# Hashed attention and a gated block on one core: weights prepared in turns, wider sums over keys, another pace

## The chip, the cores and the metric

The kernel runs on one core of a Trainium2 chip. The time is the device time of one launch in microseconds (us), lower is better. A core has five engines with queues of their own, worked off in order: PE (TensorE, matrix products into PSUM), DVE (VectorE), ACT (ScalarE), POOL (GpSimd) and SP (SyncE). Here SP and POOL only issue transfers (DMA), apart from some filling at the start. PEld in the profile is PE's loading of weights.

## The reference

Attention in which a query sees only keys of the same hash bucket (the signs of six projections), then a block `silu(x w_gate) * (x w_val)` times `w_out`. The inputs are float32 from numpy, except that the weights of the second block come out as float64, since `standard_normal * (1 / np.sqrt(...))` keeps that type.

```
batch, n_heads, seq, head_dim = (4, 8, 768, 64)
n_tokens, d_model, d_ff = (3072, 512, 1536)
mask = q_bucket[:, :, :, None] == k_bucket[:, :, None, :]
scores = np.where(mask, scale * q @ k^T, -1e9)
attn = exp(scores - max); attn = attn / (sum + 1e-09)
x = (attn @ v).transpose(0, 2, 1, 3).reshape(B * S, H * D)
g = x @ w_gate
return (g * (1 / (1 + exp(-g))) * (x @ w_val)) @ w_out
```

## The kernel before

**Attention** takes the heads in 16 pairs (4 batches of 4). A pair has 12 units: 2 halves of 384 queries by 6 chunks of 128 keys. For a unit PE makes the scores of both heads (`score`, L461), a second product of bits (`qb`, `kb`) shifts scores of other buckets down, and ACT takes the exponential into a ring of 12 tiles `A`. `attend` (L477) multiplies by `v`. DVE adds the tiles of a half (`add`, L498: one operation for the first two units, one for each later unit, 768 elements each), PE sums `acc` over the partitions (`total`, L512), ACT copies the row, SP spreads it with a transfer (`few`), DVE inverts it (`invert`), two more transfers spread it (`sums`, `r`), and `norm` (L540) multiplies. Results of batch 0 are split into three parts for the gated block (`split`, L238: `high` on ACT, `low` and `diff` on DVE); those of later batches are kept in DRAM (`xram`).

The loop over pairs (L563) writes the order out by hand: transposes on DVE for the next pair and its loads on SP, 12 scores with their sums, `total` of the pair before, `finish(rest)` (with `spread_k`, L408, on DVE), `finish(last)` (the `norm` of two pairs before), `invert`, `begin_pieces`, 6 times `attend`, the splits, 6 times `attend`, `advance_pieces`. After pair 15 it does `finish(last)` and then `total` of pair 15.

**Pieces.** The weights are float64 and are turned on the chip into three float32 parts. There are 36 pieces of 128 x 512: for each of 12 blocks of d_ff a gate and a value piece, and 12 output pieces. Preparing one takes `scale` (two on ACT), `widths` (three on DVE), `round_up` (one on ACT) and `parts` (two on DVE and a write of 768 KB to DRAM, `ram<-stage`). Three stage slots are in turn. Pieces come back for use through a ring of 7 (`bring`, L221). Attention prepares 24 pieces: two per pair in pairs 0 to 3, then one in even and two in odd pairs, none in the last.

**The gated block** is a list of groups (L207): "U" n makes one block of the hidden layer, "D" takes three blocks into the output; a D comes after every third U (U3, then D0, U4, U5, U6, D1 and so on), 48 U and 16 D over four batches. A U has four atoms: gate products and ACT's copy (L674), the correction on DVE (L680) and silu (L682), the same for the value, then the product (L684) and the split into `hid` (L685 on ACT, and on DVE, one atom later, L688 and L690). A D has six atoms, one for each 128 tokens, of nine matmuls and two operations (L721 or L719, then L724). PSUM has four tiles of two banks for all of it. Matmul lines of the gated block show as L632.

After each atom one step of preparing runs (`prepare_on`) and ACT scales ahead (`scale_ahead`). `bring` forces the preparing of a piece that it needs. Before U9 of a batch (the third from its end) all pieces left are prepared, the next batch's results are loaded (`words<-xram`, four on SP over three slots), and their 12 split steps are queued, one per atom after four empty ones: they run in D2, U10 and the first half of U11. `left` holds the last pair's `invert` and `norm`, which run at the 6th and 14th atom.

Of the kernel before, what the change touches and what calls it, by code (L numbers as in the profile page):

```python
# [8 lines left out]
FP32 = mybir.dt.float32  # L9
# [10 lines left out]
def kernel(  # L20
# [157 lines left out]
            for _ in widths(i):  # L178
                pass

    def scale_ahead():
        for i in sorted(added - rounded):
            round_up(i)
        i = progress["scaled"]
        if i < NPIECE and i < progress["kept"] + 2 and i in words:
            scale(i)

    def prepare():
        for i in range(progress["kept"], NPIECE + 1):
            if i < NPIECE and i not in added:  # L190
                load_words(i + 1)
                if i not in staged:
                    scale(i)
                yield from widths(i)
            if i > progress["kept"]:
                round_up(i - 1)
                yield from parts(i - 1)

    preparing = prepare()

    def prepare_on(n):
        for _ in range(n):
            next(preparing, None)

# [16 lines left out]
    def bring(count=1):  # L221
        for _ in range(count):
            i = len(held)
            if i == len(wanted):
                return
            what, n = wanted[i]
            at = place[what, n % NF]
            while progress["kept"] <= at:
                next(preparing)
            pool = ringp[i % sum(RINGS) >= RINGS[0]]  # L230
            held[what, n] = t = pool.tile([P, 3, PIECE], FP32R, tag="ring", name="ring")
            nc.gpsimd.dma_start(t.bitcast(FP32), ram[at].bitcast(FP32))  # L232
# [23 lines left out]
    def attention(scope):  # L256
# [102 lines left out]

        RING = 2 * NCH  # L360
        AW = HQ + 2
        ring = []
        for i in range(RING):
            t = fixed.tile([P, 2, AW], FP32, tag=f"A{i}", name="A")
            nc.gpsimd.memset(t[:, :, HQ:AW], 1.0)
            ring.append(t)
        for t in (sides["k", 0], sides["q", 0], sides["q", 1]):
            nc.gpsimd.memset(t, 0.0)

# [107 lines left out]
        def attend(u):  # L477
# [9 lines left out]
            if c == NCH - 1:  # L487
# [7 lines left out]
                    nc.scalar.activation(mean[n], ps[:, HQ : HQ + 1], AF.Copy, scale=EPS)  # L495
                nc.scalar.copy(xT[n][:, half * HQ : (half + 1) * HQ], ps[:, 0:HQ])

        def add(u):  # L498
            n, half, c = units[u]
            a = weights(u)  # L500
            if c == 1:
                acc[n, half] = att.tile([P, 2, HQ], FP32, tag="acc", name="acc", bufs=4)
                nc.vector.scalar_tensor_tensor(out=acc[n, half], in0=weights(u - 1)[:, :, 0:HQ],  # L503
                                               scalar=S * EPS / P, in1=a[:, :, 0:HQ],
                                               op0=ALU.add, op1=ALU.add)
            elif c > 1:
                nc.vector.tensor_tensor(acc[n, half], acc[n, half], a[:, :, 0:HQ], op=ALU.add)  # L507

        each = 4 * HQ // P
        sums = [dram.tile([P, each], FP32, tag=f"sums{i}", name="sums") for i in range(2)]  # L510
# [15 lines left out]
        def invert(n, few):  # L526
            nc.vector.reciprocal(few, few)
            s = sums[n % 2]
            nc.sync.dma_start(s, few)
            if n == len(pairs) - 1:  # L530
                t = spread[n].rearrange("p (x q) -> p x q", x=2)
            else:
                t = att.tile([P, 2, HQ], FP32, tag="r", name="r")
            flat = s.rearrange("p e -> (p e)").rearrange("(h x t) -> h (x t)", h=2, t=HQ)
            for h in range(2):
                nc.sync.dma_start(t[h * D : (h + 1) * D].rearrange("p x t -> p (x t)"),
                                  flat[h : h + 1].to_broadcast([D, 2 * HQ]))
            return lambda: norm(n, t)

        def norm(n, t):  # L540
            x = xT[n]
            nc.vector.scalar_tensor_tensor(out=x, in0=x, scalar=mean[n],
                                           in1=t.rearrange("p x q -> p (x q)"),
                                           op0=ALU.add, op1=ALU.mult)
            b, pr = pairs[n]
            if b:
                nc.sync.dma_start(kept_x[b, pr], x)
            else:
                splits.extend(split(x, b, pr, even_x))

        steps = front(0)
        rest = []
# [6 lines left out]
        prepare_pair(4)  # L559
        finish(rest)  # L560
        last = []
        splits = []
        for n in range(len(pairs)):  # L563
            u = 2 * NCH * n
            more = n + 1 < len(pairs)
            late = n + 1 > NP
            if n and more:
                steps = front(n + 1)
                if late:
                    prepare_pair(2)  # L570
            for i in range(2 * NCH):
                score(u + i)
                if u + i == 2:
                    prepare_pair(1)
                    finish(rest)
# [12 lines left out]
            finish(rest)  # L588
            finish(last)
            while waiting:  # L590
                last.append(waiting.pop(0)())
            begin_pieces(0 if n == len(pairs) - 1 else 2 if n < NP or n % 2 else 1)
            for c in range(NCH):
                attend(u + c)
            finish(splits)
            for c in range(NCH, 2 * NCH):
                attend(u + c)
            load(n + 2, "v")
            advance_pieces()
            if n >= len(pairs) - 3:  # L600
                bring(2 if n == len(pairs) - 1 else 1)
        finish(last)
        total(len(pairs) - 1)
        left.extend(waiting)

    left = []
# [8 lines left out]
    def gated_block(scope):  # L615
# [47 lines left out]
        def atoms_of(kind, n):  # L663
# [33 lines left out]
            else:  # L697
# [5 lines left out]
                def start(c, js):  # L703
                    if c not in tiles:
                        tiles[c] = two_banks("o")
                    t = tiles[c]
                    cols = slice(c * P, (c + 1) * P)
                    for j in js:
                        for v in range(2):
                            mm(t[:, 0], hs[j][:, v, cols], ws[j][:, v],  # L710
                               j == 0 and v == 0, j == NQ - 1 and v == 1)
                    for j in js:
                        mm(t[:, 1], hs[j][:, 2, cols], ws[j][:, 2], j == 0, j == NQ - 1)

                def end(c):
                    t = tiles.pop(c)
                    if part == 0:
# [6 lines left out]
                    nc.vector.tensor_tensor(accs[c], accs[c], t[:, 1], op=ALU.subtract)  # L724
# [5 lines left out]
                ahead = 4 if n == B * NF // NQ - 1 else 0  # L730
# [10 lines left out]
        tails = []  # L741
        splits = []
        count = [0]
        for kind, n in order:
            if kind == "U":
                b, f = divmod(n, NF)
                if f == NF - NQ and b + 1 < B:
                    while next(preparing, None):
                        pass
                    splits = [None] * 4  # L750
                    for pr in range(NP):
                        t = wordp.tile([P, PIECE, 2], I32, tag="words", name="words")
                        x = t.rearrange("p f w -> p (f w)")[:, 0:S].bitcast(FP32)
                        nc.sync.dma_start(x, kept_x[b + 1, pr])
                        splits += split(x, b + 1, pr, xs[(b + 1) % 2][pr])
            if kind == "D" and n == B * NF // NQ - 1:
                finish(tails)
            for atom in atoms_of(kind, n):
# [4 lines left out]
                if splits:  # L763
                    step = splits.pop(0)
                    if step:
                        step()
                count[0] += 1
                if left and count[0] in (6, 14):
                    left.append(left.pop(0)())
                    left[:] = [f for f in left if f]  # L770
                prepare_on(1)
                scale_ahead()

    with ExitStack() as scope:
        gated_block(scope)
# [32 lines left out]
```

## Time and profile before

| | |
|---|---|
| runs, median (lowest to highest) | 955.48 us (954.71 to 957.72) |
| the profiled execution: time, span | 955.84 us, 954.0 us |
| mean granted clock of PE | 0.993 |
| attention / gated block on PE | until 334.6 us / from 335.28 us |
| a U group, a D group on PE | 8.33 us, 12.28 us |
| DVE operation of 768 / 512 float32 columns | 0.95 to 0.96 / 0.69 us |
| ACT: L674, L682 and L685, scaling (each), round_up | 0.81, 0.85, 0.67, 0.62 us |

The span runs from the first to the last instruction of one execution; its time holds 1.8 us around that. In the timeline a row has its start, its duration, the engine and line, the operation with the tiles it writes and reads, and in brackets how long the engine stood idle before it and who released it. "PE idle" is read there; a busy PE can still be slow, which the granted clock shows (1.00 is full). Operations of DVE and ACT overlap a little in this profile, so the next can start 0.1 us before the one before is shown as ended.

### The profile page before, as it was taken

How to read it: one execution, taken by the hardware profiler on the slowest of the kernel's cores; microseconds unless marked ns; L12 is line 12 of the kernel's file. 1: busy time of each engine (PE TensorE's matmuls, PEld its weight loads, DVE VectorE, ACT ScalarE, POOL GpSimd, SP SyncE). 2: the span in 40 equal slices, each digit the busy share in tenths (PEclk: the TensorE clock that was granted, in tenths of full speed). 3: DMA queues.
4: the chain of work that ended last, by engine and by line, in shares of the span. 5: the costliest groups of instructions: out<-in, count | busy, mean ns of one | idle time of the engine just before them, and what ended most of it. 6: DMA issues, size and time to landing. Idle time of an engine off the chain costs nothing.

```text
span 954.0 us, 14590 instructions
## 1 busy us (share of the span) xinstructions
PE 926.6 (97%) x5413; PEld 726.1 (76%) x5413; DVE 672.6 (71%) x868; ACT 472.6 (50%) x882; POOL 113.2 (12%) x231
## 2 busy tenths in 40 slices
PE   8999999999999979998899999999999999999997
PEld 4444454544444479998699999999999999999996
DVE  5577899899999828796876546775646586446466
ACT  6899777887888535433341331332332421332311
POOL 3011001000111110111011111011111111110100
PEclk9999999999999999999799999999999999999999
DMA  6466767887888597879667465466654646753641
GB/s 167 123 188 175 185 163 197 223 209 186 223 231 219 190 368 264 318 273 352 241 235 287 145 263 188 160 232 235 244 207 162 226 182 203 262 196 133 243 155 67
DMA packets 135798, 203.22 MB, mean 213 GB/s; under 512 B 92912, under 2 KB 100560, under 8 KB 135728
## 3 DMA queue, kind: packets, MB, share of 16 engines
q0 software_dynamic: 27984, 145.64, 42.9%
q1 hardware_dynamic: 106944, 56.46, 22.0%
q8 instruction: 43, 0.70, 0.3%
q10 hardware_dynamic: 800, 0.20, 0.1%
q14 instruction: 27, 0.22, 0.1%
HBM read 162.01 MB, written 39.42 MB: 211 GB/s over the span
## 4 chain that ended last, share of the span: by engine, by line
PE 84%; DVE 5%; DMA 4%; ACT 3%; SPq 2%; issue 1%; DVEq 0%; ACTq 0%
PE a L632 26%; PE o L632 20%; PE sc L471 13%; PE n L632 13%; PE av L485 8%; SPq L296 2%; DVE acc L507 2%; ACT A L474 1%; PE hps L397 1%; DMA few<-row 1%; DMA r<-sums 1%; PE sum L518 1%; DMA ram<-stage 1%; PE tps L384 1%; DMA qb<-qb 1%
## 5 line engine op out<-in xcount | busy, mean ns | idle before, releaser
L632 PE MATMUL a<-xparts,ring 128*128 128x384 f32 x1536 | 283.7, 336 | 5.7 <-ACT g L674 5.1
L632 PEld LDWEIGHTS a<-xparts,ring 128*128 128x128 f32 x1536 | 269.5, 189 | 7.9 <-ACT g L674 5.4
L632 PE MATMUL o<-ring,hid 128*128 128x512 f32 x864 | 201.7, 393 | 7.6 <-ACT g L674 7.6
L632 PEld LDWEIGHTS o<-ring,hid 128*128 128x128 f32 x864 | 163.1, 190 | 42.3 <-ACT g L674 7.9
L474 ACT ACTIVATE A<-sc 128x384 f32<-128x384 f32 x384 | 155.7, 507 | 9.5 <-PE sc L471 9.5
L471 PE MATMUL sc<-qT,kT 64*128 64x384 f32 x768 | 157.9, 488 | 0.0
L632 PE MATMUL n<-xparts,ring 128*128 128x384 f32 x768 | 148.6, 334 | 0.0
L232 POOL DMA_DIRECT2D ring<-ram x144 | 75.9, 529 | 514.1 <-PE n L632 319.6
L632 PEld LDWEIGHTS n<-xparts,ring 128*128 128x128 f32 x768 | 134.5, 188 | 0.0
L507 DVE TENSOR_TENSOR acc<-acc,A 128x768 f32<-128x768 f32 x128 | 122.6, 958 | 13.6 <-DVE acc L503 0.5
L485 PE MATMUL av<-A,vraw 128*64 128x386 f32 (+1 forms) x768 | 127.7, 488 | 0.0
L680 DVE TENSOR_TENSOR v<-v,n 128x768 f32<-128x768 f32 x48 | 45.8, 954 | 102.6 <-PE n L632 97.6
L485 PEld LDWEIGHTS av<-A,vraw 128*64 128x64 f32 x768 | 53.7, 136 | 73.3 <-issue 63.8
L471 PEld LDWEIGHTS sc<-qT,kT 64*128 64x128 f32 x768 | 71.7, 187 | 46.7 <-issue 43.6
L674 ACT ACTIVATE g<-a 128x768 f32<-128x768 f32 x48 | 38.9, 810 | 129.1 <-PE a L632 129.1
L685 ACT ACTIVATE hid<-v 128x768 fp32r<-128x768 f32 x48 | 40.7, 847 | 119.3 <-DVE v L684 111.2
L682 ACT ACTIVATE g<-g 128x768 f32<-128x768 f32 x48 | 40.6, 847 | 91.9 <-DVE g L680 91.9
L724 DVE TENSOR_TENSOR o<-o 128x512 f32<-128x512 f32 x96 | 65.9, 687 | 22.0 <-ACT o L719 19.6
L471 PE MATMUL sc<-qb,kb 64*128 64x384 bf16 x384 | 69.3, 323 | 6.4 <-DVE kb L411 4.6
L688 DVE SCALAR_TENSOR_TENSOR hid<-hid,v 128x768 fp32r<-128x768 f32 x48 | 45.9, 956 | 33.1 <-ACT hid L685 33.1
L680 DVE TENSOR_TENSOR g<-g,n 128x768 f32<-128x768 f32 x48 | 45.6, 949 | 31.2 <-PE n L632 29.8
L721 DVE SCALAR_TENSOR_TENSOR o<-o 128x512 f32<-128x512 f32 x72 | 49.5, 687 | 12.0 <-PE o L632 11.4
(77 smaller groups left out, 671.8 us busy)
## 6 DMA issues: line engine op xcount, KB each, us to landing
ring<-ram POOLq DMA_DIRECT2D x144, 768.0 KB, 5.6
ram<-stage POOLq DMA_DIRECT2D x24, 768.0 KB, 4.8
ram<-stage SPq DMA_DIRECT2D x12, 768.0 KB
vraw<-in_v_dram SPq DMA_DIRECT2D x16, 384.0 KB
out_dram<-o SPq DMA_DIRECT2D x24, 256.0 KB
r<-sums SPq DMA_DIRECT2D x30, 192.0 KB
qraw<-in_q_dram SPq DMA_DIRECT2D x48, 96.0 KB
words<-in_moe_w_gate_dram POOLq DMA_DIRECT2D x9, 512.0 KB, 7.5
```

The source lines that it names most:

```text
L232: nc.gpsimd.dma_start(t.bitcast(FP32), ram[at].bitcast(FP32))
L471: nc.tensor.matmul(sc[h], x["k", n][rows, ks], x["q", n][rows, qs], start=start, stop=not start)
L474: nc.scalar.activation(weights(u)[:, h, 0:HQ], sc[h], AF.Exp, scale=SCALE * (OFF / 2 if n <= NP else 1.0))
L485: nc.tensor.matmul(ps[h * D : (h + 1) * D, 0:width], raws["v", n][:, h, c, :], a[:, h, 0:width], start=c == 0, stop=c == NCH - 1)
L507: nc.vector.tensor_tensor(acc[n, half], acc[n, half], a[:, :, 0:HQ], op=ALU.add)
L632: nc.tensor.matmul(ps, w, x, start=start, stop=stop)
L680: nc.vector.tensor_tensor(two(z), two(z), n_, op=ALU.subtract)
L682: nc.scalar.activation(z, z, AF.Silu)
L685: nc.scalar.activation(h, val, AF.Copy, scale=TOWARD / STEP)
L688: nc.vector.scalar_tensor_tensor(out=l, in0=h.bitcast(FP32), scalar=-STEP, in1=val, op0=ALU.mult, op1=ALU.add)
L721: nc.vector.scalar_tensor_tensor(out=accs[c], in0=t[:, 0], scalar=STEP + 1, in1=accs[c], op0=ALU.mult, op1=ALU.add)
L724: nc.vector.tensor_tensor(accs[c], accs[c], t[:, 1], op=ALU.subtract)
```

## The change

It edits five places:

1. `add`: the ring becomes six tiles of two units each. DVE does nothing for even units; at unit 3 it adds the first two tiles (1536 elements), at unit 5 the third tile, and then folds the two halves (768) into `acc`. The buffer `both` is new, single; `r` has one buffer instead of two.
2. Pieces per pair: `PACE`, 2 in pairs 0 to 3, 1 in 4 to 6, then 2 and 1 in turns, 0 in the last. Pair 5 makes one instead of two, so attention prepares 23.
3. Splits of batch 0 run one pair later, before the twelve `attend`; `total` of pair 15 comes before the `norm` of pair 14.
4. In the gated block each group has a `turn`: round up the piece before, scale the next, two steps of parts, three of widths, spread over its atoms by fixed counts. The forced preparing in `bring` and before U9 is gone. The x of the next batch is loaded in two pairs (at the D before U10, and at U10), and its 12 split steps run in the eight atoms of U10 and U11.
5. In the last D the correction product comes before the main one, and DVE subtracts before it adds the main one.

```diff
+    def turn():
+        old = [i for i in sorted(added) if i >= progress["kept"]]
+        new = progress["scaled"]
...
+        yield first
+        yield second
+        for i in old:
+            steps = parts(i)
+            for _ in range(2):
+                yield lambda: next(steps)
+        if new < NPIECE:
+            more = widths(new)
+            for _ in range(3):
+                yield lambda: next(more)
...
-            while progress["kept"] <= at:
-                next(preparing)
+            assert progress["kept"] > at, (i, at, progress)
...
+            if c % 2 == 0:
+                return
+            first, now = (twos[x % RING // 2][:, :, :, 0:HQ] for x in (u - 2, u))
+            if c == 3:
+                t = both[half] = att.tile([P, 2, 2, HQ], FP32, tag="both", name="both", bufs=1)
+                nc.vector.scalar_tensor_tensor(out=t, in0=first, scalar=S * EPS / P / 2, in1=now,
+                                               op0=ALU.add, op1=ALU.add)
+            elif c > 3:
+                t = both[half]
+                nc.vector.tensor_tensor(t, t, now, op=ALU.add)
+            if c == NCH - 1:
                 acc[n, half] = att.tile([P, 2, HQ], FP32, tag="acc", name="acc", bufs=4)
+                nc.vector.tensor_tensor(acc[n, half], t[:, 0], t[:, 1], op=ALU.add)
...
-                splits.extend(split(x, b, pr, even_x))
+                later.extend(split(x, b, pr, even_x))
...
+        PACE = [2] * 4 + [1] * 3 + [2, 1] * 4 + [0]
...
-            begin_pieces(0 if n == len(pairs) - 1 else 2 if n < NP or n % 2 else 1)
-            for c in range(NCH):
-                attend(u + c)
+            begin_pieces(PACE[n])
             finish(splits)
-            for c in range(NCH, 2 * NCH):
+            splits.extend(later)
+            later.clear()
+            for c in range(2 * NCH):
                 attend(u + c)
...
+        total(len(pairs) - 1)
         finish(last)
-        total(len(pairs) - 1)
...
+                    for go in (second, first) if final else (first, second):
+                        go()
...
+            b, f = divmod(n, NF if kind == "U" else NF // NQ)
+            if b + 1 < B:
+                if (kind, f) == ("D", NF // NQ - 2):
+                    load_x(b + 1, range(NP // 2))
+                elif (kind, f) == ("U", NF - NQ + 1):
+                    assert len(added) == NPIECE
+                    load_x(b + 1, range(NP // 2, NP))
...
+                if kind == "U" and f > NF - NQ:
+                    for _ in range(2 - at % 2):
+                        if splits:
+                            splits.pop(0)()
...
-                prepare_on(1)
-                scale_ahead()
+                for _ in range((1, 2, 2, 2, 1, 1)[at] if kind == "U" else (1, 2, 1, 1, 1, 1, 0, 0, 0, 0)[at]):
+                    step = next(mine, None)
+                    if step:
+                        step()
```

More of the change, by code (lines that the diff above doesn't have):

```diff
@@ L179, in advance_pieces, with first, second @@
                 pass
[L181 to L203, printed above, removed]
+    def turn():
+        old = [i for i in sorted(added) if i >= progress["kept"]]
+        new = progress["scaled"]
+        def first():
+            for i in old:
+                round_up(i)
+        def second():
+            if new < NPIECE:
+                load_words(new + 1)
+                scale(new)
+        yield first
+        yield second
+        for i in old:
+            steps = parts(i)
+            for _ in range(2):
+                yield lambda: next(steps)
+        if new < NPIECE:
+            more = widths(new)
+            for _ in range(3):
+                yield lambda: next(more)
     order = []
@@ L361, in attention @@
         AW = HQ + 2
[L362 to L366, printed above, removed]
+        twos = []
+        for i in range(RING // 2):
+            t = fixed.tile([P, 2, 2, AW], FP32, tag=f"A{i}", name="A")
+            nc.gpsimd.memset(t.rearrange("p u h q -> p (u h) q")[:, :, HQ:AW], 1.0)
+            twos.append(t)
+        ring = [t[:, i] for t in twos for i in range(2)]
         for t in (sides["k", 0], sides["q", 0], sides["q", 1]):
@@ L496, in attend @@
                 nc.scalar.copy(xT[n][:, half * HQ : (half + 1) * HQ], ps[:, 0:HQ])
+        both = {}
         def add(u):
             n, half, c = units[u]
-            a = weights(u)
-            if c == 1:
-                acc[n, half] = att.tile([P, 2, HQ], FP32, tag="acc", name="acc", bufs=4)
[L503 to L507, printed above, removed]
+            if c % 2 == 0:
[9 more added lines that the diff above has]
+            if c == NCH - 1:
+                acc[n, half] = att.tile([P, 2, HQ], FP32, tag="acc", name="acc", bufs=4)
+                nc.vector.tensor_tensor(acc[n, half], t[:, 0], t[:, 1], op=ALU.add)
         each = 4 * HQ // P
@@ L532, in invert @@
             else:
-                t = att.tile([P, 2, HQ], FP32, tag="r", name="r")
+                t = att.tile([P, 2, HQ], FP32, tag="r", name="r", bufs=1)
             flat = s.rearrange("p e -> (p e)").rearrange("(h x t) -> h (x t)", h=2, t=HQ)
@@ L561, in attention @@
         last = []
+        PACE = [2] * 4 + [1] * 3 + [2, 1] * 4 + [0]
         splits = []
+        later = []
         for n in range(len(pairs)):
@@ L707, in start, with first, second @@
                     cols = slice(c * P, (c + 1) * P)
[L708 to L713, printed above, removed]
+                    def first():
+                        for j in js:
+                            for v in range(2):
+                                mm(t[:, 0], hs[j][:, v, cols], ws[j][:, v],
+                                   j == 0 and v == 0, j == NQ - 1 and v == 1)
+                    def second():
+                        for j in js:
+                            mm(t[:, 1], hs[j][:, 2, cols], ws[j][:, 2], j == 0, j == NQ - 1)
+                    for go in (second, first) if final else (first, second):
+                        go()
                 def end(c):
                     t = tiles.pop(c)
+                    if final:
+                        nc.vector.tensor_tensor(accs[c], accs[c], t[:, 1], op=ALU.subtract)
                     if part == 0:
@@ L723, in end @@
                                                        op0=ALU.mult, op1=ALU.add)
-                    nc.vector.tensor_tensor(accs[c], accs[c], t[:, 1], op=ALU.subtract)
+                    if not final:
+                        nc.vector.tensor_tensor(accs[c], accs[c], t[:, 1], op=ALU.subtract)
                     if part == NF // NQ - 1:
@@ L728, in end @@
                         bring(NQ)
-                ahead = 4 if n == B * NF // NQ - 1 else 0
+                final = n == B * NF // NQ - 1
+                ahead = 4 if final else 0
                 for c in range(ahead):
@@ L743, in gated_block, with load_x @@
         count = [0]
-        for kind, n in order:
[L745 to L756, printed above, removed]
+        def load_x(b, prs):
+            for pr in prs:
+                t = wordp.tile([P, PIECE, 2], I32, tag="words", name="words")
+                x = t.rearrange("p f w -> p (f w)")[:, 0:S].bitcast(FP32)
+                nc.sync.dma_start(x, kept_x[b, pr])
+                splits.extend(split(x, b, pr, xs[b % 2][pr]))
+        for kind, n in order:
+            b, f = divmod(n, NF if kind == "U" else NF // NQ)
[5 more added lines that the diff above has]
+                    load_x(b + 1, range(NP // 2, NP))
+            if n == B * NF // NQ - 1 and kind == "D":
                 finish(tails)
-            for atom in atoms_of(kind, n):
+            mine = iter(turn() if progress["kept"] < NPIECE else ())
+            for at, atom in enumerate(atoms_of(kind, n)):
                 tail = atom()
@@ L762, in gated_block @@
                     tails.append(tail)
[L763 to L766, printed above, removed]
+                if kind == "U" and f > NF - NQ:
+                    for _ in range(2 - at % 2):
+                        if splits:
+                            splits.pop(0)()
                 count[0] += 1
```

## The prediction

> **What bounds the kernel now.** The page's first section comes first:
>
> ```profile
> PE 926.6 (97%) x5413; PEld 726.1 (76%) x5413; DVE 672.6 (71%) x868; ACT 472.6 (50%) x882; POOL 113.2 (12%) x231
> ```
>
> PE is the bound, and the change takes no matmul away. So it can only win back the 27.4 us in which PE idles, and the clock that long idling costs. The table of windows says where those are (columns: PE, PEld, DVE, ACT, POOL busy, granted clock, DMA share, GB/s):
>
> ```profile
> 140.00:160.00 20.00, 18.88 (x132) 9.47 (x128) 18.37 (x24) 15.71 (x38) 2.07 (x3) 1.00 0.72 172
> 200.00:220.00 20.00, 20.00 (x144) 9.62 (x144) 18.41 (x27) 16.72 (x38) 1.65 (x3) 1.00 0.81 219
> 340.00:360.00 20.00, 14.92 (x79) 14.60 (x78) 9.17 (x13) 6.33 (x9) 2.12 (x4) 0.92 0.89 341
> 440.00:460.00 20.00, 12.37 (x64) 11.38 (x64) 14.77 (x23) 7.08 (x11) 1.58 (x3) 0.81 0.84 319
> ```
>
> There are three places, and from 480 to the last group no window has any idling. PE's timeline gives each wait and its releaser:
>
> ```profile
> 117.76 0.55 PE L471 MATMUL sc<-qb,kb 64*128 64x384 bf16 x2 [1.33 <-DVE kb L411]
> 139.35 0.32 PE L471 MATMUL sc<-qb,kb 64*128 64x384 bf16 x1 [0.20 <-DMA qb<-qb]
> 161.01 0.32 PE L471 MATMUL sc<-qb,kb 64*128 64x384 bf16 x1 [0.32 <-DMA qb<-qb]
> 181.27 0.32 PE L471 MATMUL sc<-qb,kb 64*128 64x384 bf16 x1 [0.72 <-DMA qb<-qb]
> 357.28 4.44 PE L632 MATMUL a<-xparts,ring 128*128 128x384 f32 x16 [5.08 <-ACT g L674]
> 457.83 14.94 PE L632 MATMUL o<-ring,hid 128*128 128x512 f32 x54 [7.63 <-ACT g L674]
> ```
>
> Their causes, from the chain of waits and the queues' timelines:
>
> ```profile
> 344.66 10.85 DMA few<-row
> 447.37 6.19 DMA ram<-stage
> ```
>
> **Sums over keys, pace, splits a pair later (attention): -5.2 us.** In pairs 4 to 7 DVE is late. Its transposes for the next pair start at 104.68, 125.76, 147.30 and 165.69. Behind them hang SP's eight loads (about 9 us), `few` and `qb`; the scores of the next pair start 13.1 to 15.6 us after the transposes, at 117.76, 139.35, 161.01, 181.27. Later pairs repeat every 19.23 us (the chain's `av` pieces at 191.90, 211.13, 230.36). Where do the transposes fall after the change?
>
> - Per half, five sums become three. [...] *By row*, dependent sums start 1.06 apart (the chain: 151.13, 152.20, 153.26), so one fewer also saves 0.10 of handing over: 1.04 per pair. I take the row.
> - Pair 5 prepares one piece instead of two: 1.8 (three operations of `widths`) less there and 1.35 (two of `parts`) less in pair 6.
> - The splits of pairs 0 to 3 fall in pairs 3 to 6 instead of 2 to 5. DVE pays 1.9 in pair 6 that it did not pay before, but ACT no longer waits for `norm` (it did 5.7 and 4.9 us) and DVE's 0.77 before `low` goes.
>
> Played forward: the transposes at 104.68 wait for `few` of pair 3, which nothing moves, so scores stay at 117.7. Next, reciprocal 117.6, split 1.9, parts 2.7, widths 1.8: transposes at 124.0, scores 137.6. Next, `few` lands at 124.0 + 13.1 = 137.1, split 1.9, parts 1.35, widths 1.8: 142.2; the transposes allow about 156 to 158, PE's period 137.6 + 19.23 = 156.8. Next PE again, 176.1 instead of 181.27. Gain 5.2; bounds 2 (the SP loads, which remain, are slow) and 7.3 (all the excess over 19.23 from 97.05 to 181.27).
>
> **`total` ahead of the last `norm`: -6.75 us, +2.7 us.** Today SP issues `few` of pair 15 behind `xram`, which waits for `norm` of pair 14, which waits for `r` until 343.1. So `few` is issued at 344.66 and read out of `row` at 355.5. The first `hid` (L685) lies on that space, ACT stands before it, L674 behind it frees PE's PSUM tile: 5.08 idle, and then sixteen matmuls took 4.44 instead of 2.77. After the change `few` goes out once L521 has copied (335.2). Even at today's 10.85 it lands at 346. DVE still stands in `norm` until 344.2, so `sub`, the three `widths`, `sub`, product and `hid` end near 351.8, and L674 frees the tile at 352.5 against 352.2 wanted. The stall of 5.08 + 1.67 goes; a backlog stays.
>
> What is late next: ACT and DVE hand over in a loop while they are behind (hid, l, d, sub, silu, v, sub, product, hid). Today's rows give 364.09 to 371.72 = 7.6 us for it. The turns put two scalings (2 x 0.57) ahead of L674 v and `widths` ahead of l, so it is about 9.0 against PE's 8.33 per U group. Played forward with the rows' durations PE loses 0.5 + 0.7 in U2, 0.5 in U3 and 1.1 before D0. Afterwards DVE has 4.8 + 3.2 = 7.9 us of work in 8.33 (U), 8.2 + 3.2 = 11.4 in 12.28 (D), and PE's four PSUM tiles bear a lag of 4.5: nothing until D2. The 24th piece, now here, fits in the same count. Bounds: 0 and 6.
>
> **Preparing in turns: -10.3 us.** Before U9 everything left is prepared at once; ACT waits for a stage slot (the 6.19 above) with L674 behind it. Idle 7.63, and D2 takes 14.94 instead of 12.28. In turns a slot has about 15 us between its write and its reuse, against 6.2; so both go. SP's queue then holds the x loads ahead of a ram write, with slack before D3.
>
> **Splits in U10 and U11 only: +7.9 us.** Today they begin in D2 and the last `low` is early (U24 begins at 638.5):
>
> ```profile
> 635.02 0.95 DVE L246 SCALAR_TENSOR_TENSOR xparts<-xparts,words 128x768 fp32r<-128x768 f32 x1
> ```
>
> Now they are two atoms later, and each `low` on DVE stands ahead of the gate's own operation and waits for a `high` that on ACT stands behind L674. From the start of U22, by rows of 0.8 to 1.0 us: high 0 4.5, low 0 5.5; v's L674 7.9, high 1 8.7, low 1 9.7, sub 10.5, product 11.5, hid 12.4, d 14.4, low 2 15.3, sub g 16.1, silu 17.0, L674 17.7, high 3 18.5, low 3 19.5. U24 begins at 16.65 and needs low 3 in its eighth matmul, at 17.85: 1.7 idle. The last `diff` stands behind sub and product, 22.2: 0.5 more. So 2.3 each into batches 2 and 3; into batch 1, with D2's backlog and the parts of piece 35, 3.3. Bounds: 0 each, and 5.5 each if PE waited for the last `diff` before it starts.
>
> Clock: [...] The rows charge 1.67 for 5.08, nothing for gaps up to 1.3. [...] in the rows' proportion (0.33 per us of idle) 3.5 us more. [...]
>
> **The last group reordered: 0.** DVE runs without a gap from 942.83 to the end, 12 operations, and the count stays. L721 in D7 started at 657.10, when the whole chunk was done (646.82 + 5 x 2.05), not when its first part was. If the subtraction could start earlier: -0.45. Six memsets fewer, and one buffer for `r` (the norm before it is already done): nothing.
>
> **Sum.** -5.2 - 6.75 + 2.7 - 10.3 + 7.9 = -11.7. The profiled execution took 955.84 (span 954.0), so 944.1; it lies 0.36 over the median of 955.48: **943.8 us**.
>
> **Rivals.**
> 1. *The splits hide* (17%): high and low run a little earlier than I queue them, and the changes of batch cost under 1 us each. For it: my hand-over times are summed and 3% less in each operation takes a quarter off; against: L674 to `high` is one queue in order. 7 us better: 937.
> 2. *The backlog at the gate stays* (18%): `few` queues behind `r` or lands past 350, or `norm` does, or the loop of 9.0 meets a full DMA. Then 4 of the 6.75 is given back: 948.
> 3. *Slower* (6%): PE takes whole-tile waits for `xparts`, as L721 seems to for its PSUM tile. It then waits for the last `diff`: 5.5, 5.5 and 6.6 idle, [...] 1.8 to 2.2 more each: 23.4 against 19.6 won elsewhere, so 959. It decides from 6.5 us per change of batch. Against: at 22.93 PE began hashing the first half of qT while ACT was still copying the second (22.36 for 0.91, two copies), so SBUF waits go by halves.
> 4. *Attention gains nothing* (6%): SP's loads, not DVE, set the scores: 949.
>
> The forecast has 53%. A measurement here tells 0.3% (2.9 us) from no change. Range 935.5 to 951. The cases under 952.6 hold 0.94; their own spread takes 0.06 of it over that line, 0.05 within and 0.01 beyond. Faster than 952.6: 0.88; within: 0.05; slower than 958.3: 0.07.
>
> **What would show it.** Scores of pair 8 near 176; no idle over 1.5 us near 350; no gap before D2; gaps of 1.5 to 3 us where batches 1, 2, 3 begin, released by DVE's `xparts`, clock still 1.00. Wrong if those three are absent or over 5, or if pairs 4 to 8 keep their gaps.

## The result and the profile after

The changed kernel takes 947.62 us (median of four runs, 946.59 to 948.66) against 955.1 (954.62 to 957.72) for the one before beside it: ratio 0.9916 (95% interval 0.9893 to 0.994), about 7.5 us less where 11.7 were predicted. The profiled execution took 948.66 with a span of 946.8, the highest of the four. In the order of the prediction, the page's first section:

```profile
PE 927.0 (98%) x5413; PEld 720.1 (76%) x5413; DVE 665.1 (70%) x804; ACT 474.1 (50%) x882; POOL 112.4 (12%) x223
```

The matmuls are the same 5413 and so is PE's busy time (926.6 before); what became less is idling. The table of windows (PE, PEld, DVE, ACT, POOL busy, clock, DMA share, GB/s) says where:

```profile
120.00:140.00 20.00, 17.84 (x118) 8.46 (x116) 18.10 (x22) 13.73 (x31) 1.85 (x3) 0.95 0.76 186
140.00:160.00 20.00, 20.00 (x138) 10.53 (x136) 18.87 (x22) 15.82 (x36) 1.76 (x3) 0.96 0.71 174
340.00:360.00 20.00, 17.12 (x89) 16.63 (x88) 13.22 (x19) 8.68 (x13) 2.12 (x4) 0.91 0.77 306
440.00:460.00 20.00, 20.00 (x100) 17.86 (x99) 18.63 (x28) 6.88 (x11) 2.64 (x5) 1.00 0.74 277
460.00:480.00 20.00, 18.13 (x102) 17.23 (x100) 17.46 (x22) 9.54 (x13) 2.11 (x4) 1.00 0.85 336
620.00:640.00 20.00, 18.39 (x99) 16.98 (x98) 15.57 (x18) 8.46 (x11) 2.12 (x4) 1.00 0.55 181
```

From 440 to 460 PE now works throughout at full clock (12.37 us at 0.81 before). From 340 to 360 it idles 2.9 instead of 5.1, and the clock still dips. From 460 and from 620 there is idling that was not there before. PE's timeline (start, duration, then in brackets the idle before and its releaser) names the waits:

```profile
137.87 0.32 PE L473 MATMUL sc<-qb,kb 64*128 64x384 bf16 x1 [2.16 <-DMA qb<-qb]
...
351.89 4.45 PE L643 MATMUL a<-xparts,ring 128*128 128x384 f32 x16 [2.88 <-ACT g L685]
...
474.13 1.21 PE L643 MATMUL a<-xparts,ring 128*128 128x384 f32 x6
476.65 0.44 PE L643 MATMUL a<-xparts,ring 128*128 128x384 f32 x1 [1.32 <-ACT xparts L244]
477.65 1.83 PE L643 MATMUL a<-xparts,ring 128*128 128x384 f32 x9 [0.55 <-DVE xparts L247]
479.32 0.68 PE L643 MATMUL n<-xparts,ring 128*128 128x384 f32 x3
480.37 1.15 PE L643 MATMUL n<-xparts,ring 128*128 128x384 f32 x5 [0.37 <-DVE xparts L251]
```

(Lines moved by 1 to 20: L471 is now L473, the matmuls L632 are L643, L674 is L685, `hid` on ACT L685 is L696, the split's three operations are L244, L247 and L251.) The last five rows are the first product of batch 1, U12: six matmuls run, then it waits for `high`, `low` and `diff` in turn. Batches 2 and 3 begin in the same way.

With the starts of groups on PE in both traces the whole difference can be placed. A stage's time is from its first to the next stage's first matmul; "predicted" is the prediction's sum for it.

| stage | before | after | difference | predicted |
|---|---|---|---|---|
| attention, to U0 | 335.28 | 331.94 | -3.3 | -5.2 |
| U0 to D1 (with the gate, U2) | 77.49 | 75.97 | -1.5 | -4.05 |
| D1 to U10 (with the flush, D2) | 59.84 | 49.55 | -10.3 | -10.3 |
| U10 to D15 (three new batches) | 463.86 | 471.89 | +8.0 | +7.9 |
| D15 to the end | 17.53 | 17.45 | -0.1 | 0 |
| span | 954.0 | 946.8 | -7.2 | -11.7 |

Three of the five stages came out in the size that was worked out. The 4.5 us that are missing lie in two: 2.6 around 350 and 1.9 in attention. These two stages also move between executions of one kernel: the kernel before, profiled once more (below), starts U0 at 336.68 and takes 78.28 from U0 to D1, and against that trace their differences are -4.7 and -2.3.

### The profile page after: what moved, and what is told of

Read it like the earlier page. It is cut to its first block, busy times and chain, and to the rows that moved or that the text cites. A ratio compares the mean times of both kernels' runs of the same rounds, so it can differ in the third digit from the quotient of the medians.

```text
span 946.8 us, 14452 instructions
## 1 busy us (share of the span) xinstructions
PE 927.0 (98%) x5413; PEld 720.1 (76%) x5413; DVE 665.1 (70%) x804; ACT 474.1 (50%) x882; POOL 112.4 (12%) x223
## 4 chain that ended last, share of the span: by engine, by line
PE 84%; DVE 7%; ACT 4%; DMA 3%; issue 1%; SPq 0%; ACTq 0%; DVEq 0%; POOLq 0%
PE a L643 23%; PE o L643 19%; PE sc L473 15%; PE av L487 12%; PE n L643 12%; ACT A L476 1%; PE hps L399 1%; DVE xparts L247 1%; PE sum L527 1%; DMA r<-sums 1%; DMA xram<-xT 1%; DVE o L740 1%; DVE v L695 1%; DVE v L691 1%; ACT xparts L244 1%
## 5 line engine op out<-in xcount | busy, mean ns | idle before, releaser
L643 PE MATMUL a<-xparts,ring 128*128 128x384 f32 x1536 | 285.5, 336 | 7.9 <-ACT g L685 2.9
L643 PEld LDWEIGHTS a<-xparts,ring 128*128 128x128 f32 x1536 | 269.2, 188 | 12.0 <-ACT xparts L244 3.7
L643 PE MATMUL o<-ring,hid 128*128 128x512 f32 x864 | 199.5, 390 | 0.0
L643 PEld LDWEIGHTS o<-ring,hid 128*128 128x128 f32 x864 | 161.8, 188 | 33.6 <-DVE o L744 0.5
L473 PE MATMUL sc<-qT,kT 64*128 64x384 f32 x768 | 158.7, 491 | 0.0
L643 PE MATMUL n<-xparts,ring 128*128 128x384 f32 x768 | 149.7, 335 | 1.1 <-DVE xparts L251 1.1
L643 PEld LDWEIGHTS n<-xparts,ring 128*128 128x128 f32 x768 | 134.8, 188 | 2.0 <-DVE xparts L251 2.0
L685 ACT ACTIVATE g<-a 128x768 f32<-128x768 f32 x48 | 38.8, 809 | 141.3 <-PE a L643 141.3
L473 PEld LDWEIGHTS sc<-qT,kT 64*128 64x128 f32 x768 | 68.7, 188 | 50.2 <-issue 49.0
L696 ACT ACTIVATE hid<-v 128x768 fp32r<-128x768 f32 x48 | 40.7, 847 | 124.7 <-DVE v L695 118.9
L744 DVE TENSOR_TENSOR o<-o 128x512 f32<-128x512 f32 x90 | 61.8, 687 | 19.4 <-ACT o L738 17.1
L509 DVE SCALAR_TENSOR_TENSOR both<-A 128x1536 f32<-128x1536 f32 x32 | 56.1, 1754 | 18.3 <-ACT A L476 17.9
L473 PE MATMUL sc<-qb,kb 64*128 64x384 bf16 x384 | 64.7, 325 | 3.2 <-DMA qb<-qb 2.2
```

The lines of the kernel that those rows point to most:

```text
L473: nc.tensor.matmul(sc[h], x["k", n][rows, ks], x["q", n][rows, qs], start=start, stop=not start)
L509: nc.vector.scalar_tensor_tensor(out=t, in0=first, scalar=S * EPS / P / 2, in1=now, op0=ALU.add, op1=ALU.add)
L643: nc.tensor.matmul(ps, w, x, start=start, stop=stop)
L696: nc.scalar.activation(h, val, AF.Copy, scale=TOWARD / STEP)
```

## The experiments

All are edits of the changed kernel unless they say otherwise. "Ratio" is to the kernel before.

### Are the new idles at changes of batch the splits' late start?

In the prediction's row of the kernel before, the last `low` of batch 2 starts 3.3 us ahead of U24 (638.34). After the change U24 begins at 626.27, and DVE starts that `low` 1.9 us behind it:

```profile
628.16 0.96 DVE L247 SCALAR_TENSOR_TENSOR xparts<-xparts,words 128x768 fp32r<-128x768 f32 x1 [1.47 <-ACT xparts L244]
```

In the experiment the first four of the twelve split steps go back to D2's atoms, where six had been; the rest stays in U10 and U11.

```diff
-                if kind == "U" and f > NF - NQ:
-                    for _ in range(2 - at % 2):
-                        if splits:
-                            splits.pop(0)()
+                now = 0
+                if (kind, f) == ("D", NF // NQ - 2):
+                    now = int(at > 1)
+                elif kind == "U" and f > NF - NQ:
+                    now = (1, 2, 1, 2)[at] if f == NF - NQ + 1 else 1
+                for _ in range(now):
+                    if splits:
+                        splits.pop(0)()
```

> The changed kernel with the split steps of the next batch begun in the D before U10 (one in each of its last four atoms, then 1, 2, 1, 2 in U10 and 1, 1 in U11), nothing else. My theory (each low waits on DVE for a high queued behind L685 on ACT, so the last one comes late): the loss from the end of D2 to the start of the last D, 472.05 us against the 463.86 of the kernel before, goes back to 464 to 466, the gaps where batches 1, 2 and 3 begin go, and the span falls by 6 to 8 us, to about 940 (ratio to before about 0.984). Rival (the loss there has another cause, such as late loads of x or the order of the loads on SP, which stay as they are): the gaps stay and the time moves by less than 2 us.

937.73 us (936.73 to 939.11), ratio 0.9846 (0.9818 to 0.9874), span 937.2. From U10 to D15 it takes 463.87, against 471.89 with the change and 463.86 before it: all 8.0 us are back, and the interval of the ratio is clear of that of the change. On DVE the last `low` of batch 1 starts at

```profile
471.91 0.95 DVE L247 SCALAR_TENSOR_TENSOR xparts<-xparts,words 128x768 fp32r<-128x768 f32 x1
```

and PE takes U12, from 472.62 on, without a break:

```profile
472.62 2.93 PE L643 MATMUL a<-xparts,ring 128*128 128x384 f32 x16
475.39 1.55 PE L643 MATMUL n<-xparts,ring 128*128 128x384 f32 x8
```

So the cost was the later start of the steps; the new loads of x, which stay as they are, cost nothing here. The other 1.6 us of the span came in attention, which this edit doesn't touch (below).

### What does `hid` wait for at the gate?

The prediction let the stall of 5.08 go, since `few` would be early. In the chain of waits of the changed kernel (start, duration, what) another transfer stands there:

```profile
330.41 9.41 DMA r<-sums
...
339.93 1.03 DVE xT L551
...
340.97 9.14 DMA xram<-xT
...
350.30 0.84 ACT hid L696
351.14 0.71 ACT g L685
```

`few` was issued at 331.91, as predicted. But `norm` of pair 14 (L551) ends at 340.96, `xram` copies its result to DRAM until 350.1, and the first `hid` waits for it. Its tile has nothing to do with that result; it is the first write to a pool that was opened where attention's pools were. Three kernels try this.

**Another place for the pool alone.** `hid`'s pool is opened before that of the split results.

```diff
+        hidp = scope.enter_context(tc.tile_pool(name="hidp", bufs=4))
         rest = scope.enter_context(tc.tile_pool(name="odd_x_rest", bufs=1))
         xs = [dict.fromkeys(range(NP), even_x), {**dict.fromkeys(range(NP - 1), rest), **odd_x}]
-        hidp = scope.enter_context(tc.tile_pool(name="hidp", bufs=4))
```

> The changed kernel with the pool of hid allocated before that of the other x parts, so that the first hid lies on the space of qT and kT and not on that of xT; nothing else. My theory (the first write of hid waits until the transfer of xT of pair 14 has read it, 340.97 to 350.1): the wait of 5.8 us in front of the first hid goes, hid comes at about 347.2, the idle of 2.88 and the slow matmuls behind it (4.45 instead of 2.77) go, and the span falls by 3 to 5 us. Rival (the lateness of norm, DVE's backlog and the turns of preparing alone hold U2 up): idle of 1.5 us or more stays before U2 and the span falls by less than 1.5 us.

That failed: 947.15 us (946.66 to 948.85), ratio 0.9933 (0.9911 to 0.9955), span 946.7. ACT's timeline has the same wait:

```profile
349.35 0.84 ACT L696 ACTIVATE hid<-v 128x768 fp32r<-128x768 f32 x1 [5.74 <-DMA xram<-xT]
```

**The order at the end of attention undone**, `norm` of pair 14 before `total` of pair 15 again:

```diff
-        total(len(pairs) - 1)
         finish(last)
+        total(len(pairs) - 1)
```

> The changed kernel with the norm of pair 14 ahead of the total of pair 15 again, as it was before. As the prediction had it (few, queued behind norm, was what held the first hid): the start of U2 comes 4 us or more later and the span grows by 3 to 5 us. As the trace after says (the transfer of xT is as late as few was): few, issued some 0.5 us behind it, lands at about 351, and the span grows by 0 to 1.5 us only.

948.38 us (947.99 to 950.11), ratio 0.9946 (0.9929 to 0.9963). U0 to D1 takes 78.93 against 75.97. `few` is issued behind `xram` once more, and ACT waits for it, 2 us longer than for `xram`:

```profile
351.02 0.84 ACT L696 ACTIVATE hid<-v 128x768 fp32r<-128x768 f32 x1 [7.69 <-DMA few<-row]
```

PE's idle in U2 grows from 2.88 to 4.77: U2 begins 22.1 us after U0 instead of 19.95, and the rest of the 3.0 is a clock that falls further (0.83 instead of 0.91 from 340 to 360). So the reorder is worth 3.0 in the changed kernel, 2.1 of it the wait itself, and not the 6.75 that the prediction let go: it takes one of two late transfers away. The interval of the ratio overlaps that of the change, so this rests on the traces.

**The pool over others.** `hid`'s pool is opened last, behind the gate's, the ring's and the output's.

```diff
+        gatep = scope.enter_context(tc.tile_pool(name="gatep", bufs=2))
         ringp.append(scope.enter_context(tc.tile_pool(name="late_ring", bufs=RINGS[1])))
...
-        hidp = scope.enter_context(tc.tile_pool(name="hidp", bufs=4))
-        gatep = scope.enter_context(tc.tile_pool(name="gatep", bufs=2))
         outp = scope.enter_context(tc.tile_pool(name="outp", bufs=1))
+        hidp = scope.enter_context(tc.tile_pool(name="hidp", bufs=4))
```

> The changed kernel with the pools of the gated block allocated in another order (gate tiles, late ring, x parts, output, hid last), so that hid lies on the space of the tiles A and of none that a late transfer reads; nothing else. Theory: the pool of hid waits for the transfers that read any tile of the attention pools under it (moving it over qT and kT still left it over row and xT further up). Then the first hid comes at about 347 with no wait on xram, the idle before U2 falls from 2.9 to under 1 us and the matmuls behind it take 2.8 again; from the start of U0 to that of D1 it takes 71.5 to 73 us instead of 76.0, span down by 3 to 4.5. Rival (DVE's backlog is what holds U2): over 75 us from U0 to D1.

944.02 us (943.69 to 944.66), ratio 0.9884 (0.9858 to 0.9909), span 942.3. ACT:

```profile
344.83 0.84 ACT L696 ACTIVATE hid<-v 128x768 fp32r<-128x768 f32 x1 [2.64 <-DVE v L695]
```

The transfer is gone from `hid`'s wait, though `xram` was still issued in that trace, at 338.66. PE, one product later:

```profile
351.36 3.06 PE L643 MATMUL a<-xparts,ring 128*128 128x384 f32 x16 [0.48 <-ACT v L685]
```

U0 to D1 takes 73.09. Seven U of 8.33 and one D of 12.28 are 70.6, so 2.5 us of backlog remain: the 2.7 of the prediction. Order of pools, with no other edit, is worth 2.9 us here by the traces (the intervals of the two ratios just overlap); it shows that the wait belongs to the place in memory and not to the data. Which attention tile lay under `hid` in each order wasn't read out, so why the first move of the pool failed is not shown.

### Attention: which part does what, and what is the 2.16 us wait for `qb`?

The rows that the prediction shows for pairs 6 and 7 are the shorter of two waits. Ahead of them the scores had waited for DVE's `kb`, 1.28 us at 138.83 and 1.49 at 160.37. PE's list of waits (total, times, longest) has both, here in the second profile of the kernel before,

```profile
PE sc L471 <- DVE kb L411: 4.5, 4, 1.5
PE sc L471 <- DMA qb<-qb: 2.9, 5, 1.2
```

and in the profile after:

```profile
PE sc L473 <- DMA qb<-qb: 2.2, 1, 2.2
PE sc L473 <- DVE kb L413: 1.0, 2, 0.5
```

So it is mostly the wait for DVE that went; a wait for the transfer stays. Three kernels put one part alone into the kernel before, with one execution each: the wide sums,

```diff
+            elif c > 3:
+                t = both[half]
+                nc.vector.tensor_tensor(t, t, now, op=ALU.add)
+            if c == NCH - 1:
                 acc[n, half] = att.tile([P, 2, HQ], FP32, tag="acc", name="acc", bufs=4)
+                nc.vector.tensor_tensor(acc[n, half], t[:, 0], t[:, 1], op=ALU.add)
```

> The kernel before with the sums over two units in one operation (and the single buffer of r), nothing else. By the prediction's row DVE is 1.04 us shorter per pair; but if SP's chain of loads, few and qb sets the scores of pairs 5 to 8, as the prediction's steps have it, that time alone moves nothing: gated block begins at 334 to 335.5 (before: 335.28). Rival (DVE's sums set them): 1 us per pair, begins at 331 to 332.

one piece instead of two in pair 5,

```diff
-            begin_pieces(0 if n == len(pairs) - 1 else 2 if n < NP or n % 2 else 1)
+            begin_pieces(0 if n == len(pairs) - 1 else 1 if n == 5 else 2 if n < NP or n % 2 else 1)
```

> The kernel before with one piece instead of two in pair 5, nothing else (the gated block prepares the 13th piece by its own order, so its stall before D2 may grow by 1 to 3 us). Theory (the transposes of pairs 7 and 8 stand behind the pieces): scores of pair 7 and 8 begin 1.8 and 3 to 4 us sooner, gated block begins at 331.5 to 333. Rival (pieces hide): it begins within 0.7 us of 335.28.

and the splits one pair later.

```diff
-                splits.extend(split(x, b, pr, even_x))
+                later.extend(split(x, b, pr, even_x))
...
             finish(splits)
-            for c in range(NCH, 2 * NCH):
+            splits.extend(later)
+            later.clear()
+            for c in range(2 * NCH):
```

> The kernel before with the splits of batch 0 one pair later and ahead of the attends, nothing else. Theory: pairs 4 and 5 win 0.8 us each, since ACT's high no longer waits for norm, and pair 6 pays 1.9 for a split it did not have: gated block begins within 1 us of 335.28. Rival (ACT's wait of 5 us for norm was what delayed the scores): it begins before 333.5.

Beside them the kernel before ran once more, to see how far its own attention wanders:

> The kernel before, profiled once more, to see how far attention's end wanders without any edit: the gated block began at 335.28 in the first profile; the four executions of the changed kernel's attention began it between 329.4 and 331.9. If the wandering is of that size, it begins here between 333.5 and 336.

| kernel | time | U0 starts |
|---|---|---|
| before; once more | 955.84; 958.0 | 335.28; 336.68 |
| wide sums alone | 955.47 | 333.00 |
| pace alone | 955.42 | 333.29 |
| splits later alone | 953.26 | 334.30 |

Against 335.28 the parts give -2.3, -2.0 and -1.0, against 336.68 each 1.4 more. The wide sums fell between theory and rival, the pace 0.3 short of its range, the splits within theirs. The kernel before alone moves by 1.4 between two executions, and the one with the pace alone lost 1.8 us to the clock from 100 to 140 (0.95 and 0.96, after waits of 1.34 and 0.90), so one execution each doesn't rank the parts. The wider operation in the groups of the profile after (count, busy time, mean ns, idle before and what ended it):

```profile
L509 DVE SCALAR_TENSOR_TENSOR both<-A 128x1536 f32<-128x1536 f32 x32 | 56.1, 1754 | 18.3 <-ACT A L476 17.9
```

How long it would take was the author's estimate, since the kernel before has no sum of 1536 columns. With L513 (1758 ns) and L516 (958) the sums of a half are busy for 1.754 + 1.758 + 0.958 = 4.47 us, against 0.941 + 4 x 0.958 = 4.77 before (L503, L507): 0.61 less per pair. The rest of the prediction's 1.04 was to be handing over (1.06 from start to start against 0.96). All three parts together have more executions than one, because six of the other kernels leave attention's code as the change has it: U0 starts at 331.94 in the profile after, at 330.37, 331.04, 330.53 and 329.43 in the first three experiments and the one with the pool opened last, and at 328.64 and 329.29 in the two runs with stops for PE (below). The mean of the seven is 330.18; that of the two of the kernel before is 335.98. That is -5.8, and the profiled execution is the slowest of the seven. What it lost shows in the rows above: scores of pair 6 wait 2.16 us for `qb`, and in the windows from 120 to 160 the clock falls to 0.95 and 0.96 (0.05 x 20 + 0.04 x 20 = 1.8 us). In the first experiment the same place idles less,

```profile
137.99 0.32 PE L473 MATMUL sc<-qb,kb 64*128 64x384 bf16 x1 [1.15 <-DMA qb<-qb]
```

and U0 starts 1.6 us sooner there. `qb` is a small transfer (`spread_q`) behind SP's loads for the next pair: in the profile after those go out from 125.03, `few` at 135.22 and `qb` at 135.92. The next kernel issues it on ACT's queue:

```diff
             def spread_q():
-                nc.sync.dma_start(bits["q", n][high], bits["q", n][low])
+                nc.scalar.dma_start(bits["q", n][high], bits["q", n][low])
```

> The changed kernel with the transfer qb<-qb (spread_q) issued on ACT's queue and not on SP's, where it stands behind eight loads and few; nothing else. My theory (SP's queue sets the scores of pair 6): the idle of 2.16 us before 137.87 goes, and with it the clock of 0.95 and the 1.67 us that the scores behind it take longer; the gated block begins 3 to 4 us sooner, span down by 3 to 4. Rival (DVE's kb, 1 us earlier, or ACT, which issues one more transfer a pair, takes the place of qb): span down by less than 1.5 us, or up.

946.14 us (945.08 to 947.6), ratio 0.9934 (0.9911 to 0.9956), span 944.4. The waits of PE list no `qb` any more, and where the 2.16 stood the scores run on:

```profile
135.17 0.92 PE L473 MATMUL sc<-qT,kT 64*128 64x384 f32 x4
135.97 0.34 PE L473 MATMUL sc<-qb,kb 64*128 64x384 bf16 x2
136.13 0.82 PE L473 MATMUL sc<-qT,kT 64*128 64x384 f32 x4
```

U0 starts at 328.43, 3.5 us sooner than in the profile after and 1.7 sooner than the mean of the seven. But one of the seven starts it at 328.64 without this edit, and the interval of the ratio overlaps that of the change: the wait for `qb` is gone, and what that is worth by itself is not separated from chance. The span gains only 2.4, since in that execution the first change of batch cost 0.9 us more (see the clock, below).

### How long may PE idle before its clock falls?

The prediction expected the clock at 1.00 through gaps of 1.5 to 3 us, an estimate of its author that no trace had shown, and met two idles of that length, 2.16 and 2.88, with a clock of 0.95 and 0.91 in their windows. Two runs of one kernel measure it by itself: in eight of the D groups PE is stopped before the fourth of six chunks by a small product, a chain of 1 to 8 dependent copies on ACT and a second small product (they add work, so the time of the whole kernel says nothing).

```diff
+                def idle(c):
+                    t = tiles[c] = two_banks("o")
+                    mm(t[0:1, 0, 0:128], hs[0][:, 0, 0:1], ws[0][:, 0, 0:128], True, True)
+                    nc.scalar.activation(nap[0:1, 0:128].bitcast(FP32R), t[0:1, 0, 0:128], AF.Copy)
+                    for _ in range(lengths[n]):
+                        nc.scalar.activation(nap.bitcast(FP32R), nap, AF.Copy)
+                    mm(t[0:1, 0, 0:128], nap.bitcast(FP32R)[:, 0:1], nap.bitcast(FP32R)[:, 0:128], True, True)
```

> The changed kernel with a stop for PE before the fourth chunk of D5, D6, D7, D9, D10, D11, D13 and D14: a small product, 1 to 8 dependent operations on ACT, a small product that waits for them. It measures what an idle costs beyond itself: the time of that D less 12.28 less the idle. [...] as the trace after suggests (1.67 after 2.16[...]), the step comes between 1.8 and 2.9 us and is about 1.7 us whatever the length up to 5 us.

> The same kernel again, for the idles near the edge: if the cost there depends on when the idle falls, idles of 1.8 to 3 us cost differently in the two executions; those below and above cost the same.

From the second small product to the next group PE needs 6.25 us at full clock:

| idle, us | 1.02 | 1.68 | 2.34 | 3.00 | 3.66 | 4.32 | 4.98 | 5.64 |
|---|---|---|---|---|---|---|---|---|
| first run | 6.24 | 6.24 | 6.28 | 6.25 | 8.77 | 7.59 | 7.89 | 7.67 |
| second run | 6.28 | 6.27 | 6.25 | 7.80 | 7.89 | 7.76 | 7.85 | 7.79 |

At 3.00 the two runs differ. PE's timeline in the first,

```profile
724.87 0.22 PE L645 MATMUL o<-nap 128*1 128x128 f32 x1 [3.00 <-ACT nap L741]
724.93 6.36 PE L645 MATMUL o<-ring,hid 128*128 128x512 f32 x27
```

and in the second:

```profile
724.50 0.26 PE L645 MATMUL o<-nap 128*1 128x128 f32 x1 [3.00 <-ACT nap L741]
724.56 7.91 PE L645 MATMUL o<-ring,hid 128*128 128x512 f32 x27
```

The same 27 matmuls after the same idle take 1.55 us more in one than in the other. Above 3.00 every one of the eight idles costs 1.3 to 2.5 us, no more for 5.64 than for 3.66.

Shorter idles can cost too when several follow each other. Where batch 1 begins, the profile after has idles of 1.32 and 0.55, and the nine matmuls behind them take 1.83 us. The first run with stops has the same two idles there, long before its first stop:

```profile
474.57 3.25 PE L645 MATMUL a<-xparts,ring 128*128 128x384 f32 x9 [0.56 <-DVE xparts L247]
```

Seven of the traces have this pair of idles. In two, the profile after and the one with `norm` first, it cost no clock. In five (the pool apart, the pool last, `qb` on ACT and both runs with stops) the nine matmuls take 2.4 to 3.3 us, the clock from 468 to 484 is 0.89 instead of 1.00, and in the three of them without stops the way from U10 to U22 is 0.9 us longer (153.06 against 152.14). The idles of 0.71, 0.55 and 0.35 where batches 2 and 3 begin were free in all seven.

### Three edits together

The splits from D2 on, `hid`'s pool last and `qb` on ACT's queue, each as above.

> The changed kernel with three of the edits tried above together: split steps from the D before U10, pools in the order that puts hid over the tiles A, qb<-qb issued by ACT. They act in three different stretches, so the gains should add: 8 us between D2 and the last D, 2.9 us between U0 and D1, 1 to 3.5 us in attention: span 931 to 935, ratio to before 0.975 to 0.979. If they don't add (for example because the split steps in D2 meet the turns with less slack), 937 or more.

934.25 us (933.79 to 935.51, six runs), ratio 0.9791 (0.9761 to 0.9821), span 932.6: the median is 13.4 us below that of the changed kernel. The two weren't timed beside each other; by their ratios the three edits are worth 1.3%. The page's first section and a window where the gate was:

```profile
PE 921.3 (99%) x5413; PEld 716.8 (77%) x5413; DVE 664.1 (71%) x804; ACT 472.9 (51%) x882; POOL 112.2 (12%) x223
```

```profile
340.00:360.00 20.00, 19.37 (x110) 18.46 (x109) 16.54 (x23) 10.87 (x17) 2.64 (x5) 1.00 0.96 349
```

U0 starts at 328.83, U0 to D1 takes 72.92, U10 to D15 463.87. PE's busy time falls too, by 5.7 us with the same matmuls: the mean granted clock is 1.000 instead of 0.996, and no product is cut off and begun again at a change of batch. As an estimate from the rows, these are 0.004 x 947 = 3.8 and 3 x 0.8 = 2.4. Of the span 11.3 us are left in which PE is not busy.

## Why the prediction was right, and where it fell short

**The flush** (-10.3): right in size, and in cause as far as the trace goes. D2 takes 12.28 again (14.78 from start to start before, not the 14.94 of its row; the other 0.16 lies ahead of it), the idle of 7.63 is gone, and ACT's waits for `ram<-stage` between 400 and 500, 6.2 us before, are gone from its list. No run has the turns alone.

**The splits in U10 and U11 only** (+7.9, measured +8.0): right in cause, and in the sum partly by luck. Per batch 3.3, 2.3 and 2.3 were predicted and 3.1, 2.5 and 2.5 measured, but not from the same terms. For batches 2 and 3 the prediction had idles of 2.2, for the last `low` and `diff`; the trace has 0.71, 0.55 and 0.35, together 1.6, and the first and longest is for `high` on ACT. At batch 1 they are 2.2. The stages are longer than the idles by 0.8 per batch, and for that the prediction had no term. It agrees with the rows: where the product is cut off and begun again, a single matmul shows 0.44 us, and inside a run it takes 2.77 / 16 = 0.17; three breaks of 0.27 make 0.8. In this execution the clock stayed full, as predicted; in five others the same idles at batch 1 lowered it. The rival in which PE waits for the whole tile falls by the row of six matmuls ahead of the first wait, and the one in which the splits hide by the first experiment.

**The gate** (-6.75 + 2.7): here the prediction failed, in the step "The stall of 5.08 + 1.67 goes". It knew that `hid` lies on space that attention's transfers read, named `few`, and saw `xram` only as what `few` stood behind. But `xram` reads such space too. Put ahead of `norm`, `few` stops being last, and `xram` is: issued at 340.97, read at 350.1. The stall shrinks from 5.08 to 2.88 and the 1.67 of clock stays; swapping the order is worth 3.0. The backlog of 2.7 was right, as the kernel without the wait shows (2.5), but in the changed kernel it is mostly hidden in the stall: U0 to D1 lost 6.9 us over 70.6 before and loses 5.4 after. The rival "the backlog at the gate stays" put the time at 948, close to the 947.62 measured, but by luck: only 2.6 of the 4 us it gives back are missing at the gate, and none of its reasons is the one found. `few` went out early, `norm` ended at 340.96, and the wait isn't the loop's.

**Attention** (-5.2): near in the mean of seven traces (-5.8), 1.9 short in the profiled one. Its steps fit less well than its sum. Scores of pairs 5 to 8 were put at 117.7, 137.6, 156.8 and 176.1, and came at 116.08, 137.87, 158.78 and 178.01. The first was to stay because nothing moved its transposes; they started at 103.88 instead of 104.68. The 1.6 us won there went again in pair 6, in the wait for `qb`. From pair 6 to pair 7 it took 20.9 us instead of 19.23, and that is the step that failed: the clock. The prediction counted nothing for it and expected "clock still 1.00" with gaps of 1.5 to 3 us; that was its author's estimate, which no trace had shown. The idle of 2.16 for `qb` and that of 2.88 at the gate are of that length, and both cost clock: 1.7 to 1.8 us in the first case, by these starts and by the windows, and in the second 1.7, since U2's second product begins at 357.76, 5.87 after the first, against 4.16 in the groups that follow. The loss in proportion (0.33 per us of idle), which the prediction also named, would have been 0.7 and 1.0; neither fits. The four times of the changed kernel fit this too: the runs at a mean clock of 0.998 and 0.999 took 946.65 and 946.59, those at 0.993 and 0.996 took 948.6 and 948.66.

**The tail** (0, measured -0.1): right; DVE runs its last 12 operations without a gap from 935.71 to 943.71, 8.0 us, as it did from 942.83 on before.

## What to carry to other kernels

When a stall is put down to a transfer that still reads the space of a new tile, list every transfer that reads that space and when each ends: taking the last one away can only uncover the next (5.08 us of idle became 2.88 here), and opening pools in another order may remove the wait without touching the work (2.9 us here). When small steps on two engines wait for each other in order, moving them by a few atoms can cost as much as a removed stall brings: 8.0 us here, against 10.3 for the flush. Playing the rows forward by hand found the cost, its size partly by luck. Before idling is called free of clock cost, look at the rows after idles of that length in the same kernel, more than once: at 3.00 us two runs here differ by 1.55.

## What was not expected of the hardware

The length of idle from which PE's clock falls is not sharp here. Stops of up to 2.34 us by small products were free in both runs and stops of 3.66 to 5.64 cost 1.3 to 2.5 us in both; at 3.00 one run lost 1.55 and the other nothing. In the kernel itself 2.16 and 2.88 cost about 1.7 each, and two idles in a row, 1.31 and 0.55, lowered the clock in five traces of seven (0.89 from 468 to 484). Nor does the length set the loss: 1.67 after 5.08, 1.4 to 1.5 after 5.64, but 2.5 after one of the two stops of 3.66 and after the 7.63 of the kernel before (its D2 takes 14.78 from start to start instead of 12.28). What decides up to 3.00 us was not found.

A transfer whose result nobody on PE's path waits for stopped PE for microseconds: `few` for 5.08 in the kernel before, `xram` for 2.88 in the changed one. They take 10.85 and 9.14 us from issue to landing at the gate, where the DMA share is 0.89 and 0.77, and `hid`, placed over what they read, starts at 355.69 and 350.30, 0.2 us after each has landed.
